# Linear attention and a two-layer MLP in one kernel: batch 1's kv between its transposes, its numerator a slot sooner, phi of batch 2 sooner, the first scale and two matmuls in halves

## The chip, the cores and the metric

The kernel runs on one core of a Trainium2 chip. The metric is device microseconds (us) of one execution. A program on one core has one value for each execution; executions of one kernel here lie within about 1.5 us of each other, and all runs quoted were in the fast state at a granted TensorE clock of 0.997 to 1.0. A profile is of one execution, and its span (first to last instruction) is about 1.8 us shorter than the time of that execution.

Names: PE is TensorE, ACT is ScalarE, DVE is VectorE, POOL is GpSimd, SP is the engine that issues most DMAs. L366 is line 366 of the kernel's source; the same statement has other line numbers in some variants (L387 is L392 where five lines were added above it, and the changed kernel's two matmuls in halves are at L577).

## The reference, cut to what matters

```python
def _attn_ref(q, k, v):                       # 8 batches, 8 heads, 576 tokens, 64 wide
    phi = lambda x: np.where(x > 0, x, np.exp(x) - 1.0) + 1.0
    q_p, k_p = phi(q), phi(k)
    kv = np.einsum('bhsd,bhse->bhde', k_p, v)
    z = np.sum(k_p, axis=2)
    num = np.einsum('bhsd,bhde->bhse', q_p, kv)
    den = np.einsum('bhsd,bhd->bhs', q_p, z)[..., None] + 1e-06
    return num / den

def _moe_ref(x, w_in, w_out):                 # x: 4608 tokens x 512
    h = x @ w_in                              # layer 1, 512 -> 2048
    g = h - np.tanh(h)
    return g @ w_out                          # layer 2, 2048 -> 512
```

The attention output of all heads, transposed to 4608 x 512, is the input of the MLP.

## The kernel before

The MLP goes in nine blocks of 512 tokens: 64 matmuls of layer 1 (L366), then 64 of layer 2 (L387), and so on. The attention of the following batches is put between these matmuls in "slots": the lists `s1[fi]` run after group `fi` of layer 1 (four matmuls each), and `s2[s]` after step `s` of layer 2 (four matmuls each). PE starts its matmuls in program order, so a slot whose input is not ready stops all matmuls behind it: at 39.17 us in the kernel before, the transposes wait 0.56 us for DVE, and the products behind them come only after them.

The parts that the change and the argument touch:

```python
# batch 0, before layer 1 of block 0
b0_spread((0, 2), 0)      # 1/den of head pairs 0 and 2, spread over partitions by PE (L240)
b0_scale(0, ns0, 0)       # xT = numerator x 1/den, on DVE (L244)
b0_scale(2, ns0, 1)
b0_num(1, ns0)
def open2():              # called after the first two matmuls of layer 1
    b0_spread((1, 3), 2); b0_scale(1, ns0, 2); b0_scale(3, ns0, 3)
...
def spread1(h):           # batch 1: 1/den spread by PE (L354), two scales on DVE (L359)
def num1():               # batch 1: numerator by PE, five copies to SBUF by ACT (L344, L346)
def a_split(b):           # 1/den split into bf16 parts: w, on DVE (L295 to L298)
def a_spread(b):          # later batches: 1/den goes to DRAM (ds) and comes back broadcast (rdb), by SP
def gate(qT):             # POOL reads the last element of qT, so the loads after it wait for the transposing DMA
...
# block c == 0
s2[7].append(lambda: (a_qT_pe(1, 0, side), a_qT_pe(1, 1, side), a_kv(1, side)))   # L164, L164, L177
s2[8].append(lambda: b0_scale_rest(side))
s2[9].append(lambda: a_den(1, side))
s2[10].append(lambda: (num1(), a_split(1)))
s2[11].append(lambda: spread1(0))
s2[12].append(lambda: q2(0))                         # phi of q, batch 2
s2[13].append(lambda: (spread1(1), q2(1)))
s2[14].append(lambda: q2(2))                         # ... and the transposing DMA of q, batch 2
s2[15].append(lambda: a_kphi(2, 0))                  # phi of k, batch 2
# blocks c >= 1, n1 = c + 1, n2 = c + 2
s1[7 if c == 1 else 5].append(lambda: a_kv_cols(n1, attn))                        # kv, L199
s1[10 if c == 1 else 8].append(lambda: (a_den(n1, attn), a_spread(n1)))
for p in range(NP + 1):
    s2[(11 if c == 1 else 9) + p].append(lambda p=p: a_num(n1, p))                # L317 on PE, L328 on DVE
s1[0].append(lambda: (gate(qT_t[n1]), load_k(n2), load_q(n2), load_v(n2)))
```

In layer 2 of block 0, steps 8 to 11 read the third quarter of `w_out`, which is loaded by POOL's DMA queue behind batch 1's q and v.

Of the kernel before, what the change touches and what calls it, by code (L numbers as in the profile page):

```python
# [18 lines left out]
def kernel(  # L19
# [9 lines left out]
    nc = tc.nc  # L29
# [127 lines left out]
    def a_qT_pe(b, i, banks, on=None):  # L157
        if i == 0:
            new_qT(b)
        for n in range(2):  # L160
            j0, j1 = ((0, 5), (5, 9))[n]
            ps = banks().bitcast(BF16).rearrange("p (j t) -> p j t", t=128)
            for j in range(j0, j1):
                nc.tensor.transpose(ps[:, j - j0, :], qp_t[b][:, i, j].rearrange("p h d -> p (h d)"), ident)  # L164
            src = ps[:, 0:j1 - j0, :]
            dst = qT_t[b][:, i, j0:j1].rearrange("p j g t -> p j (g t)")
            if (on or "AV")[n] == "A":
                nc.scalar.copy(dst, src)
            else:
                nc.vector.tensor_copy(dst, src)  # L170
# [69 lines left out]
                nc.tensor.matmul(ps_all[:, 4 + t, 128 * (n0 + n):128 * (n0 + n) + 128],  # L240
                                 sel[r, p].rearrange("p h e -> p (h e)"), rden_t[0][r, 0:128], start=True, stop=True)

    def b0_scale(p, ns, n):
        nc.vector.tensor_mul(  # L244
            xT[:, p, 0:512].rearrange("p (j t c) -> p t j c", j=8, t=4),
            ns[:, p, 0:8].rearrange("p j (t c) -> p t j c", t=4),
            ps_all[:, 4:8, 128 * n:128 * n + 128].rearrange("p t (j c) -> p t j c", c=16))

    def b0_rest():

# [225 lines left out]
    b0_kv(1)  # L476
    b0_kz(1)
    b0_spread((0, 2), 0)
    b0_scale(0, ns0, 0)
    b0_scale(2, ns0, 1)  # L480
    b0_num(1, ns0)

# [19 lines left out]
    for c in range(NC):  # L502
        gT = gpool.tile([128, NF, 512], BF16, name="gT")
        n1, n2 = c + 1, c + 2
        s1 = {i: [] for i in range(16)}
        s2 = {i: [] for i in range(16)}
        if c == 0:
            side = Banks([4, 5, 6, 7])
            sub = {}

            def spread1(h):
                sub["bp"] = a_spread_pe(1, 4, (2 * h, 2 * h + 1))
                for p in (2 * h, 2 * h + 1):
                    a_scale(1, p, sub["ns"], sub["bp"], 144 * (p % 2))

            def num1():
                sub["ns"] = new_ns(1)
                for p in (NP, 0, 1, 2, 3):
                    a_num_copy(1, sub["ns"], p, side)

            s1[11].append(lambda: a_kphi(1, 0))
            s1[13].append(lambda: a_kphi(1, 1))
            s2[3].append(lambda: a_qphi(1, 0))
            s2[4].append(lambda: (a_qphi(1, 1), load_q(2), load_k(2), load_v(2)))
            s2[0].append(prepare)
            s2[7].append(lambda: (a_qT_pe(1, 0, side), a_qT_pe(1, 1, side), a_kv(1, side)))
            s2[8].append(lambda: b0_scale_rest(side))
            s2[9].append(lambda: a_den(1, side))
            s2[10].append(lambda: (num1(), a_split(1)))
            s2[11].append(lambda: spread1(0))  # L530

            def q2(n):
                if n == 0:
                    sub["q"] = [phi_pieces(2, q_t, qp_t, "qp", i) for i in range(2)]
                if n < 2:
                    for f in sub["q"][n][:2]:
                        f()
                else:
                    for x in sub["q"]:
                        x[2]()  # L540
                    a_qT_dma(2)

            s2[12].append(lambda: q2(0))
            s2[13].append(lambda: (spread1(1), q2(1)))
            s2[14].append(lambda: q2(2))
            s2[15].append(lambda: a_kphi(2, 0))
        elif n1 < B:
            s1[7 if c == 1 else 5].append(lambda: a_kv_cols(n1, attn))
            s1[10 if c == 1 else 8].append(lambda: (a_den(n1, attn), a_spread(n1)))
            for p in range(NP + 1):  # L550
                s2[(11 if c == 1 else 9) + p].append(lambda p=p: a_num(n1, p))
        if c == 1:
            s1[1].append(lambda: a_kphi(2, 1))
            for i in range(2):
                s1[3].append(lambda i=i: a_vp(2, i))
        if c >= 1 and n2 < B:

            s1[0].append(lambda: (gate(qT_t[n1]), load_k(n2), load_q(n2), load_v(n2)))
            d = 2
            s2[d].append(lambda: a_kphi(n2, 0))  # L560
            s2[d + 2].append(lambda: a_kphi(n2, 1))
            s2[d + 4].append(lambda: a_qphi(n2, 0))
            s2[d + 6].append(lambda: (a_qphi(n2, 1), a_qT_dma(n2)))
            for i in range(2):
                s2[14 + i].append(lambda i=i: a_vp(n2, i))
        if c == 0:

            first = Banks([4, 5, 6, 7, 0, 1, 2, 3])
            hs = [ps_all[:, n, :] for n in range(4)]
            order = [((0, 0), (0, 1)), ((2, 0), (2, 1), (0, 2), (0, 3), (2, 2), (2, 3)),  # L570
                     [(p, fi) for p in (1, 3) for fi in range(4)]]
            seen = [0] * 4
            for n, part_ in enumerate(order):
                if n == 1:
                    open2()
                for p, fi in part_:
                    l1mm(c, fi, hs[fi], p, seen[fi])  # L577
                    seen[fi] += 1
            for fi in range(4):
                l1act(fi, hs[fi], gT)  # L580
        for fi in range(4 if c == 0 else 0, NF):
            h = first() if c == 0 else dense()
            for p in range(NP):
                l1mm(c, fi, h, p, p)
            if c == 0:
                l1act(fi, h, gT)
            elif fi % 2:
                n = dense.order[(dense.n - 1) % 6]
                l1act2(fi - 1, ps_all[:, n - 1:n + 1, :], gT)
            for f in s1[fi]:  # L590
                f()
        os_ = {}
        for s in range(16):

            (g, i) = divmod(s, 4) if c == 0 else (s % 4, s // 4)
            if g == 0:
                os_[i] = ps_all[:, i, :] if c == 0 else dense()
            if c == NC - 1 and i == 3:

                if g == 0:  # L600
                    o2 = dense()
                    for o, f in ((os_[i], slice(0, 384)), (o2, slice(384, DM))):
                        for fi in range(NF):
                            nc.tensor.matmul(o[:, f], gT[:, fi, 384:512], w_out_sb[:, fi, f],  # L604
                                             start=(fi == 0), stop=(fi == NF - 1))
                        evac(c, i, o, f.start, f.stop)
                continue
            l2mm(gT, os_[i], i, 4 * g, 4 * g + 4)
            if g == 3:
                evac(c, i, os_[i])  # L610
            for f in s2[s]:
                f()
# [30 lines left out]
```

## Time and profile before

| | before |
|---|---|
| time, median of 4 runs with the result's pair | 294.95 us (294.70 to 295.49) |
| span of the profiled execution | 293.2 us |
| PE busy | 285.2 us, 97% |
| PE idle waits that the profile names, before 60 us | 3.8 us, 1.2 of it at the very start |
| layer 1 of block 1 begins (first L366 after 51 us) | 51.30 us |
| den of batch 1 to its first spread, start to start | 3.94 us (43.32 to 47.26) |

How to read it: PE is the bound, so what counts are the waits of PE, and where PE stands at a few landmarks. Ends of matmuls are modelled, so I count from start to start: a 512-column matmul takes 0.216 us, a step or a group of four 0.863.

### The profile page before, as it was taken

What the parts mean: (1) busy time and instruction counts of PE and PEld (TensorE: products, weight loads), DVE (VectorE), ACT (ScalarE), POOL (GpSimd) and SP (SyncE); (2) the same over time, 40 slices, a digit from 0 to 9 for tenths busy, and PEclk for the clock granted to TensorE, in tenths of its full rate; (3) what the DMA queues carried; (4) which work ended last, traced back from release to release, by engine and by line L of the source; (5) the groups of instructions that cost most, each with busy time, mean ns of one, the idle gap of its engine ahead of it and who ended that gap; (6) DMA issues with size and microseconds to landing.
All of it is one profiled execution on the core that took longest, in us unless ns stands there. A gap on an engine that the chain in (4) does not pass through costs nothing.

```text
span 293.2 us, 4504 instructions
## 1 busy us (share of the span) xinstructions
PE 285.2 (97%) x1801; PEld 134.3 (46%) x1801; DVE 174.6 (60%) x265; ACT 139.6 (48%) x168; POOL 33.3 (11%) x55
## 2 busy tenths in 40 slices
PE   8899999999999999999999999999999999999994
PEld 2544453454444444444444445444444444444443
DVE  4759857887567764786478646865581456106600
ACT  4938536947344643455246524661552155126411
POOL 8673030030030003000300020000000000000000
PEclk9999999999999999999999999999999999999999
DMA  6999999998999758955895669667117310131032
GB/s 101 194 204 212 208 207 216 200 145 153 234 163 185 160 118 139 218 117 129 136 223 127 139 134 183 134 154 143 38 24 178 73 36 0 38 84 24 0 74 72
DMA packets 39077, 38.94 MB, mean 133 GB/s; under 512 B 16336, under 2 KB 33808, under 8 KB 38288
## 3 DMA queue, kind: packets, MB, share of 16 engines
q0 software_dynamic: 17552, 18.35, 38.6%
q1 hardware_dynamic: 21344, 20.17, 30.3%
q8 instruction: 14, 0.23, 0.3%
q10 hardware_dynamic: 160, 0.13, 0.1%
q14 instruction: 7, 0.06, 0.1%
HBM read 43.91 MB, written 9.55 MB: 182 GB/s over the span
## 4 chain that ended last, share of the span: by engine, by line
PE 79%; DMA 11%; issue 7%; POOL 2%; DVE 0%; ACT 0%; POOLq 0%
PE ps_all L387 37%; PE ps_all L366 36%; DMA qraw<-in_q_dram 6%; DMA w_in_sb<-in_moe_w_in_dram 3%; PE ps_all L199 2%; DMA kraw<-in_k_dram 2%; PE ps_all L317 2%; PE ps_all L604 1%; PE ps_all L276 1%; POOL qraw L90 0%; ACT e L134 0%; POOL kraw L93 0%; DVE qp L136 0%; POOL v L93 0%; POOL w_out_sb L115 0%
## 5 line engine op out<-in xcount | busy, mean ns | idle before, releaser
L366 PE MATMUL ps_all<-xT,w_in_sb 128*128 128x512 bf16 x576 | 128.0, 379 | 0.3 <-DVE xT L244 0.3
L387 PE MATMUL ps_all<-w_out_sb,gT 128*128 128x512 bf16 x560 | 127.8, 379 | 0.0
L373 DVE TENSOR_TENSOR gT<-ps_all,th 128x1024 bf16<-128x1024 f32 x64 | 77.9, 1218 | 59.8 <-ACT th L372 59.8
L372 ACT ACTIVATE th<-ps_all 128x1024 f32<-128x1024 f32 x64 | 65.5, 1024 | 57.0 <-PE ps_all L366 47.1
L366 PEld LDWEIGHTS <-w_in_sb 128*128 128x128 bf16 x576 | 55.3, 98 | 66.6 <-issue 0.6
L387 PEld LDWEIGHTS <-gT 128*128 128x128 bf16 x560 | 54.1, 98 | 64.3 <-issue 0.3
L396 ACT COPY osb<-ps_all 128x512 f32<-128x512 f32 (+1 forms) x36 | 20.9, 583 | 73.4 <-PE ps_all L387 54.2
L328 DVE TENSOR_TENSOR xT<-ps_all,rdb 128x512 bf16<-128x512 f32 x24 | 16.3, 689 | 13.4 <-PE ps_all L317 11.2
L134 ACT ACTIVATE e<-qraw 128x1152 bf16<-128x1152 bf16 x16 | 18.5, 1162 | 6.9 <-DMA qraw<-in_q_dram 6.9
L134 ACT ACTIVATE e<-kraw 128x1152 bf16<-128x1152 bf16 x15 | 17.5, 1166 | 0.2 <-DMA kraw<-in_k_dram 0.2
L136 DVE TENSOR_TENSOR qp<-e,r 128x1152 bf16<-128x1152 bf16 x16 | 12.0, 757 | 7.8 <-ACT e L134 7.2
L136 DVE TENSOR_TENSOR kp<-e,r 128x1152 bf16<-128x1152 bf16 x15 | 11.4, 759 | 8.3 <-ACT e L134 7.5
L383 POOL COPY g<-qT 1x1 bf16<-1x1 bf16 x5 | 1.2, 240 | 120.6 <-DMA qT<-qp 120.6
L378 DVE TENSOR_TENSOR gT<-ps_all,th 128x512 bf16<-128x512 f32 x16 | 10.3, 685 | 2.4 <-ACT th L377 1.7
L377 ACT ACTIVATE th<-ps_all 128x512 f32<-128x512 f32 x16 | 9.2, 598 | 4.3 <-PE ps_all L366 3.1
L317 PE MATMUL ps_all<-qT,kz 128*128 128x512 bf16 x28 | 10.1, 379 | 0.0
L444 PE MATMUL ps_all<-zero 128*128 128x512 bf16 x29 | 8.8, 463 | 1.2 <-DVE zero L405 1.2
L135 DVE TENSOR_SCALAR r<-qraw 128x1152 bf16<-128x1152 bf16 x16 | 7.3, 453 | 2.2 <-DMA qraw<-in_q_dram 2.2
L199 PE MATMUL ps_all<-vp,kp 64*128 64x136 bf16 x216 | 7.4, 220 | 0.4 <-POOL g L383 0.4
L199 PEld LDWEIGHTS <-kp 64*128 64x128 bf16 x216 | 6.4, 94 | 3.0 <-issue 2.1
L285 DVE RECIPROCAL rden<-den 128x144 f32<-128x144 f32 x7 | 7.4, 1053 | 0.2
L394 DVE COPY osb<-ps_all 128x128 f32<-128x128 f32 x1 | 0.3, 292 | 11.6 <-PE ps_all L604 11.6
(82 smaller groups left out, 121.7 us busy)
## 6 DMA issues: line engine op xcount, KB each, us to landing
out_dram<-osb SPq DMA_DIRECT2D x70, 128.0 KB
rdb<-ds SPq DMA_DIRECT2D x12, 576.0 KB
kraw<-in_k_dram POOLq DMA_DIRECT2D x7, 576.0 KB, 7.1
qraw<-in_q_dram POOLq DMA_DIRECT2D x7, 576.0 KB, 9.0
v<-in_v_dram POOLq DMA_DIRECT2D x7, 576.0 KB, 12.2
w_out_sb<-in_moe_w_out_dram POOLq DMA_DIRECT2D x4, 512.0 KB, 16.4
w_in_sb<-in_moe_w_in_dram POOLq DMA_DIRECT2D x6, 256.0 KB, 8.6
qraw<-in_q_dram POOLq DMA_DIRECT2D x2, 288.0 KB, 4.6
```

The costliest lines, as they stand in the source:

```text
L134: return (lambda: nc.scalar.activation(e, x, AF.Exp), lambda: nc.vector.tensor_scalar(r, x, 0.0, 1.0, ALU.max, ALU.add), lambda: nc.vector ...
L136: lambda: nc.vector.tensor_tensor(y, e, r, ALU.min))
L199: nc.tensor.matmul(ps[hg][:, i, :], kp[r, i, j].rearrange("p h d -> p (h d)"), vp[r, i, j, :], start=(j == 0), stop=(j == J - 1))
L317: nc.tensor.matmul(ps, kz[:, p // 2, p % 2, 0:128], qT[:, p % 2, 0:8, p // 2, :], start=True, stop=True)
L328: nc.vector.tensor_mul(xT[:, p, S * b:S * b + 512].rearrange("p (j t c) -> p j t c", j=8, t=4), ps.rearrange("p j (t c) -> p j t c", t=4), ...
L366: nc.tensor.matmul(h, w_in_sb[:, 2 * (p % 2) + p // 2, fi * 128:(fi + 1) * 128], xT[:, p, c * 512:(c + 1) * 512], start=(n == 0), stop=(n ...
L372: nc.scalar.activation(th, h, AF.Tanh)
L373: nc.vector.tensor_sub(gT[:, fi:fi + 2, :], h, th)
L377: nc.scalar.activation(th, h, AF.Tanh)
L378: nc.vector.tensor_sub(gT[:, fi, :], h, th)
L387: nc.tensor.matmul(o, gT[:, fi, i * 128:(i + 1) * 128], w_out_sb[:, fi, :], start=(fi == 0), stop=(fi == NF - 1))
L396: nc.scalar.copy(osb[:, f0:f1], o[:, f0:f1])
```

## The change

Its intent: (1) the first 1/den scale and the first two matmuls of layer 1 in halves of 256 tokens, so that PE starts sooner; (2) kv of batch 1 between its two blocks of transposes, so that PE has work while the second half of phi is made; (3) the numerator of batch 1 one slot sooner, so that its copies are done by the spread; (4) phi of batch 2 in earlier slots, and the kv product of batch 2 one group later.

```diff
--- before.py
+++ after.py
@@ -240,11 +240,11 @@
                 nc.tensor.matmul(ps_all[:, 4 + t, 128 * (n0 + n):128 * (n0 + n) + 128],
                                  sel[r, p].rearrange("p h e -> p (h e)"), rden_t[0][r, 0:128], start=True, stop=True)
 
-    def b0_scale(p, ns, n):
+    def b0_scale(p, ns, n, j0=0, j1=8):
         nc.vector.tensor_mul(
-            xT[:, p, 0:512].rearrange("p (j t c) -> p t j c", j=8, t=4),
-            ns[:, p, 0:8].rearrange("p j (t c) -> p t j c", t=4),
-            ps_all[:, 4:8, 128 * n:128 * n + 128].rearrange("p t (j c) -> p t j c", c=16))
+            xT[:, p, 64 * j0:64 * j1].rearrange("p (j t c) -> p t j c", j=j1 - j0, t=4),
+            ns[:, p, j0:j1].rearrange("p j (t c) -> p t j c", t=4),
+            ps_all[:, 4:8, 128 * n + 16 * j0:128 * n + 16 * j1].rearrange("p t (j c) -> p t j c", c=16))
 
     def b0_rest():
 
@@ -476,7 +476,9 @@
     b0_kv(1)
     b0_kz(1)
     b0_spread((0, 2), 0)
-    b0_scale(0, ns0, 0)
+
+    b0_scale(0, ns0, 0, 0, 4)
+    b0_scale(0, ns0, 0, 4, 8)
     b0_scale(2, ns0, 1)
     b0_num(1, ns0)
 
@@ -523,36 +525,33 @@
             s2[3].append(lambda: a_qphi(1, 0))
             s2[4].append(lambda: (a_qphi(1, 1), load_q(2), load_k(2), load_v(2)))
             s2[0].append(prepare)
-            s2[7].append(lambda: (a_qT_pe(1, 0, side), a_qT_pe(1, 1, side), a_kv(1, side)))
+            s2[7].append(lambda: (a_qT_pe(1, 0, side), a_kv(1, side), a_qT_pe(1, 1, side)))
             s2[8].append(lambda: b0_scale_rest(side))
-            s2[9].append(lambda: a_den(1, side))
-            s2[10].append(lambda: (num1(), a_split(1)))
+            s2[9].append(lambda: (a_den(1, side), num1(), a_split(1)))
             s2[11].append(lambda: spread1(0))
 
-            def q2(n):
-                if n == 0:
-                    sub["q"] = [phi_pieces(2, q_t, qp_t, "qp", i) for i in range(2)]
-                if n < 2:
-                    for f in sub["q"][n][:2]:
-                        f()
-                else:
-                    for x in sub["q"]:
-                        x[2]()
-                    a_qT_dma(2)
-
-            s2[12].append(lambda: q2(0))
-            s2[13].append(lambda: (spread1(1), q2(1)))
-            s2[14].append(lambda: q2(2))
-            s2[15].append(lambda: a_kphi(2, 0))
+            qs, ks = [], []
+
+            def exp2(pieces, src, store, name, i):
+                pieces.append(phi_pieces(2, src, store, name, i))
+                pieces[i][0]()
+
+            def rest2(f):
+                f[1]()
+                f[2]()
+
+            s2[11].append(lambda: (exp2(qs, q_t, qp_t, "qp", 0), rest2(qs[0])))
+            s2[12].append(lambda: exp2(qs, q_t, qp_t, "qp", 1))
+            s2[13].append(lambda: (spread1(1), exp2(ks, k_t, kp_t, "kp", 0), rest2(qs[1]), a_qT_dma(2)))
+            s2[14].append(lambda: rest2(ks[0]))
         elif n1 < B:
-            s1[7 if c == 1 else 5].append(lambda: a_kv_cols(n1, attn))
+            s1[8 if c == 1 else 5].append(lambda: a_kv_cols(n1, attn))
             s1[10 if c == 1 else 8].append(lambda: (a_den(n1, attn), a_spread(n1)))
             for p in range(NP + 1):
                 s2[(11 if c == 1 else 9) + p].append(lambda p=p: a_num(n1, p))
         if c == 1:
             s1[1].append(lambda: a_kphi(2, 1))
-            for i in range(2):
-                s1[3].append(lambda i=i: a_vp(2, i))
+            s1[3].append(lambda: (a_vp(2, 0), a_vp(2, 1)))
         if c >= 1 and n2 < B:
 
             s1[0].append(lambda: (gate(qT_t[n1]), load_k(n2), load_q(n2), load_v(n2)))
@@ -573,7 +572,12 @@
             for n, part_ in enumerate(order):
                 if n == 1:
                     open2()
-                for p, fi in part_:
+                for x in range(2 if n == 0 else 0):
+                    for p, fi in part_:
+                        nc.tensor.matmul(hs[fi][:, 256 * x:256 * x + 256], w_in_sb[:, 0, fi * 128:(fi + 1) * 128],
+                                         xT[:, p, 256 * x:256 * x + 256], start=(x == 0), stop=False)
+                        seen[fi] = 1
+                for p, fi in part_ if n else ():
                     l1mm(c, fi, hs[fi], p, seen[fi])
                     seen[fi] += 1
             for fi in range(4):
```

## The prediction

> **What bounds the kernel now.** I read the page first: busy time by engine, then the chain that ended last.
>
> ```profile
> PE 285.2 (97%) x1801; PEld 134.3 (46%) x1801; DVE 174.6 (60%) x265; ACT 139.6 (48%) x168; POOL 33.3 (11%) x55
> ...
> PE 79%; DMA 11%; issue 7%; POOL 2%; DVE 0%; ACT 0%; POOLq 0%
> ```
>
> TensorE (PE) is the bound: busy 97% of a span of 293.2 us, and the windows view gives 229.00 us of PE busy in the 229 us from 60 to 289. Nothing that lies after 60 us can therefore be gained; a change of order is worth only the PE idle time that it closes before that. So I read next what PE waited for (us in total, times, longest):
>
> ```profile
> PE ps_all L444 <- DVE zero L405: 1.2, 1, 1.2
> PE ps_all L164 <- DVE qp L136: 0.8, 2, 0.6
> PE ps_all L354 <- ACT ns L344: 0.7, 1, 0.7
> PE ps_all L221 <- DMA v<-in_v_dram: 0.4, 1, 0.4
> PE ps_all L199 <- POOL g L383: 0.4, 1, 0.4
> PE ps_all L366 <- DVE xT L244: 0.3, 1, 0.3
> ```
>
> Four of these are what the change is aimed at: the second block of transposes of batch 1 (L164, 0.56 us of its 0.8), the spread of 1/den of batch 1 (L354), the kv product of batch 2 (L199) and the first matmul of layer 1 (L366). Together some 2.0 us, 0.7% of the time: the most that could be had at face value. The timeline of PE (start us, us, what) places them, and shows what comes after each:
>
> ```profile
> 15.44 0.61 PE L231 MATMUL ps_all<-qT,kz 128*128 128x512 bf16 x2
> 16.38 0.59 PE L366 MATMUL ps_all<-xT,w_in_sb 128*128 128x512 bf16 x2 [0.33 <-DVE xT L244]
> 16.98 0.73 PE L240 MATMUL ps_all<-rden,sel 32*128 32x128 f32 x16
> ...
> 37.94 0.68 PE L164 MATMUL ps_all<-ident,qp 128*128 128x128 bf16 x9
> 39.17 0.68 PE L164 MATMUL ps_all<-ident,qp 128*128 128x128 bf16 x9 [0.56 <-DVE qp L136]
> 39.78 1.66 PE L177 MATMUL ps_all<-v,kp 64*128 64x192 bf16 x36
> 41.37 1.04 PE L387 MATMUL ps_all<-w_out_sb,gT 128*128 128x512 bf16 x4
> ```
>
> The reader should see that PE does not idle at 41.37. But the product there is the first that reads the third quarter of w_out, and the view of that tile, for the load issued at 23.01 us, says:
>
> ```profile
> L115 POOL DMA_DIRECT2D w_out_sb<-in_moe_w_out_dram x1: 762/762/762, 23.0 to 23.0; - x1
> ...
> DMA to landing us min/median/max: 18.3/18.3/18.3
> ```
>
> 23.0 + 18.3 = 41.3 us: it lands (41.32 in the trace) 0.05 us before PE gets there. The same view for batch 1's v, issued at 22.28, gives 16.5, so it lands at 38.80. The windows view has the DMA share at 1.2 in 31:38 and 38:41.4: the queue is full, so neither arrives sooner because PE does.
>
> **What the Trainium skill says.** "TensorE: Matmul & The Clock Gate", section "Wait — 56ns, not 53.3ns?", gives a start-to-start of about 215.7 ns for a warm 512-column matmul. The trace agrees: 62 matmuls of L366 from 17.64 to 31.03 are 0.216 us each. I count in starts, since ends are modelled. "PSUM — Partial Sum Buffer", section "PSUM bank collisions raise a hardware error", says that a dependency is put between two engines on one bank and quadrant even at different columns. The trace agrees: the second spread (L240) starts at 16.98, 0.06 after the second scale, which reads other columns of the same banks, ends at 16.92. The TensorE page's section "Architectural detail" calls ACT and DVE strict FIFO queues, so an early phi stands ahead of what comes later in program order; DVE's rows show that order throughout. "DMA: Bandwidth & Descriptors", section "Issuing engines are not separate DMA queues", has all DMAs share 16 engines, which fits the loads landing one after another 2.5 to 3 us apart.
>
> **Part 1, the first scale and two matmuls in halves.** DVE now has two scales from 15.64, 605 ns apart, the first ending at 16.32, and L366 starts at 16.38. A 256-column multiply from PSUM (L263, L225) takes 420 ns against 687, and the pipeline overlaps some 80, so I estimate halves ending at 16.06 and 16.40, and the scale of pair 2 at 16.99 instead of 16.92, since 2 x 0.34 is 0.07 more than 0.605. PE could start its first half at about 16.11. But the next PE instructions are the spread of pairs 1 and 3, and those wait for the scale of pair 2. They start 0.06 after it: at 17.05 in place of 16.98. The earlier start buys nothing, and layer 1 begins 0.07 us later. Even that does not last: batch 1's kv waits for v until 38.85 either way.
>
> **Part 2, kv between the transposes.** The 9 transposes start at 37.94 to 38.0 and are followed by kv after 9 x 0.056 + 0.15 = 0.65, at about 38.6. v lands at 38.80, so kv starts at about 38.85, an idle of 0.2. kv takes 41.37 - 39.78 = 1.59, to 40.44; the second transposes (qp of half 1 is ready at 39.11, the copies of half 0 have freed their banks at about 39.45) take 0.55, to 41.0. PE would be at the w_out product 0.37 sooner than 41.37, and waits for the landing at 41.32: it starts at about 41.34. Gain 0.03 us of the 0.72 that the starts show lost. The wait moves from DVE to two DMAs.
>
> **Part 3, the five copies of batch 1's numerator one slot earlier.** Before: den starts at 43.32, the numerator at 44.56, ACT's copies end at 47.20 (2.64 after the numerator starts), and the spread starts at 47.26 where an unheld PE would be at 46.50. After: den at 43.29, the numerator 0.37 later at 43.66, copies done at 46.30. PE gets to the spread at 46.47. The other input, w, comes from DVE: den 0.31, reciprocal 1.05 and four splits (0.23, 0.37, 0.23, 0.37), which end 3.22 after den starts, now as before: 43.29 + 3.22 = 46.51. So the spread starts at about 46.56: gain 0.70 us, w and no longer ns being the last wait (about 0.1).
>
> **Part 4, phi of batch 2 sooner, kv of batch 2 one step later.** Batch 2's kv starts at 58.74, 0.75 after the matmul before it, where its counterparts in later batches start 0.31 after: 0.43 us lost. The profile names the gate copy on POOL, which ends at 58.73, but kv does not read it. The first half of vp does: DVE's copies at L189 start at 58.23, 0.82 for two, so half 0 ends at about 58.7. They are late because DVE is: from 51.02 it has the phi of q half 1, of k half 0 and half 1 and two 1.22 us subtractions in a row. With most phi done before layer 1, and layer 1 of block 1 from 50.61, I work DVE out in order: scales of pairs 2 and 3 until 50.9, phi of q half 1 until 52.0, of k half 0 until 53.1, then the subtractions, k half 1 and vp, half 0 done at 57.5. kv, now after 9 groups, is due at 50.61 + 9 x 0.863 = 58.4. No wait: gain 0.43.
>
> What could be lost: the exponential of q half 0 stands on ACT before the evacuations, and q of batch 2 lands at 46.67 (issued 38.78, 7.9 to landing), so it runs 46.7 to 47.9, as the first evacuation comes due; the four then end by 52.4, the third at 51.8 where layer 1 wants its bank at 52.3. On DVE the phi of q half 0 goes before the scales of pairs 2 and 3: 50.2 and 50.9, wanted at 51.0 and 51.25. Both fit, with 0.3 to 0.5 us to spare.
>
> **Sum.** 0 + 0.03 + 0.67 + 0.43 = 1.13 us, of 295.09: 293.96. I say 293.9, for w_out may land a little sooner in other executions.
>
> **Rivals.** (a) All gaps close at face value, DMA not in the way: for it, the waits view shows no w_out wait; against it, the landing times. Then 0.37 more, perhaps 0.2 from part 1: 293.4. (b) Phi too early: its wait for q on ACT, or its place before the scales on DVE, holds layer 1 of block 1 for 0.3 to 0.6 us: about 294.4. For it, margins of 0.3; against it, that each stands worked out as met. (c) The loads for batch 3, released about 1.5 us sooner since the transposing DMA is issued sooner, disturb later stages. Against it: no PE idle after 60 us and DMA shares of 0.59 there; no change.
>
> **Range and chances.** Before spreads over 294.81 to 295.49, 0.7 us; the rivals span 293.4 to 294.4. I take 293.2 to 294.8. A change of 2% is 5.9 us, three times all the idle in question, and no step here can cost that; 98% within.
>
> **What would show it.** Right: spread of pairs 1 and 3 at 17.0 to 17.1 despite a first matmul near 16.1; kv of batch 1 held by v until about 38.85; the product at s = 8 held by DMA until about 41.3; first spread of batch 1 near 46.6, released by w; layer 1 of block 1 from about 50.6; no gap before batch 2's kv at about 58.4. Wrong: the product at s = 8 starting near 41.0 (rival a), or gaps in layer 1 of block 1, or behind ACT's first evacuations (rival b).

## More of the kernel before

One more place turned out to matter, which the prediction did not look at: the numerators of batch 2 in layer 2 of block 1. The timeline of PE before (start us, us, what) has them at

```profile
77.66 0.38 PE L317 MATMUL ps_all<-qT,kz 128*128 128x512 bf16 x1
...
78.73 0.38 PE L317 MATMUL ps_all<-qT,kz 128*128 128x512 bf16 x1
...
79.85 0.38 PE L317 MATMUL ps_all<-qT,kz 128*128 128x512 bf16 x1
```

and the timeline of DVE shows when the multiply of the first of them by 1/den could run, and what it waited for:

```profile
79.10 1.89 DVE L328 TENSOR_TENSOR xT<-ps_all,rdb 128x512 bf16<-128x512 f32 x3 [2.26 <-DMA rdb<-ds]
```

The first numerator starts at 77.66, but 1/den (rdb) lands only at 79.1. The numerators use two PSUM banks in turn, so the third has to wait until DVE has read the first. Unheld they stand 1.08 us apart (one step and one numerator); here the third is 1.12 after the second: 0.04 us lost. The kernel before stands right at the edge of this wait.

## The result, and the profile after

The changed kernel takes 293.67 us (median of 4 runs, 293.54 to 293.97) against 294.95 for the kernel before (4 runs). The ratio is 0.9956, with a 95% interval of 0.9938 to 0.9973: clearly a little faster. Ratios here are the mean time of one kernel's fast runs over that of the other's of the same rounds, so they are not quite the ratio of the medians. The predicted 293.9 and its range hold.

The page after, busy time and the chain that ended last:

```profile
PE 284.2 (97%) x1775; PEld 134.5 (46%) x1803; DVE 174.8 (60%) x266; ACT 139.7 (48%) x168; POOL 33.1 (11%) x55
...
PE 75%; DMA 18%; POOL 2%; issue 1%; SPq 1%; DVE 1%; ACT 1%; DVEq 0%; POOLq 0%
```

DMA's share of the chain went from 11% to 18%: the chain now runs over loads. (PE's count is lower only because some matmul records are missing from the trace; a start-to-start of 0.43 is one of those.) What PE waited for, after:

```profile
PE ps_all L444 <- DVE zero L405: 1.2, 1, 1.2
PE ps_all L221 <- DMA v<-in_v_dram: 0.4, 1, 0.4
PE ps_all L240 <- DVE xT L244: 0.2, 1, 0.2
PE ps_all L366 <- issue: 0.2, 1, 0.2
```

The four waits that the change aimed at are gone, and one is new, of the spread (L240) for the scale. The last line is a missing record. The timeline of PE after:

```profile
16.12 0.71 PE L577 MATMUL ps_all<-xT,w_in_sb 128*128 128x256 bf16 x4
17.05 0.73 PE L240 MATMUL ps_all<-rden,sel 32*128 32x128 f32 x16 [0.22 <-DVE xT L244]
...
38.01 0.67 PE L164 MATMUL ps_all<-ident,qp 128*128 128x128 bf16 x9
38.60 1.66 PE L177 MATMUL ps_all<-v,kp 64*128 64x192 bf16 x36
40.20 0.68 PE L164 MATMUL ps_all<-ident,qp 128*128 128x128 bf16 x9
40.93 1.02 PE L387 MATMUL ps_all<-w_out_sb,gT 128*128 128x512 bf16 x3
...
46.16 0.30 PE L354 MATMUL ps_all<-w,sel 32*128 32x144 bf16 x8
...
50.20 7.93 PE L366 MATMUL ps_all<-xT,w_in_sb 128*128 128x512 bf16 x35
58.06 1.24 PE L199 MATMUL ps_all<-vp,kp 64*128 64x136 bf16 x36
```

and the view of the tile w_out for the load of its third quarter, issued at 23.05 us:

```profile
L115 POOL DMA_DIRECT2D w_out_sb<-in_moe_w_out_dram x1: 760/760/760, 23.1 to 23.1; - x1
...
DMA to landing us min/median/max: 17.8/17.8/17.8
```

It lands at 40.89, and step 8 starts at 40.93, with no idle shown: the modelled ends of the transposes cover the wait. Layer 1 of block 1 begins at 50.20 in place of 51.30, and kv of batch 2 comes without a gap. By 61 us PE is 1.54 us ahead (den of batch 2 at 61.06, before 62.60). But the span is only 1.3 us shorter. The difference is in layer 2 of block 1, where PE shows no named wait:

```profile
76.12 0.38 PE L317 MATMUL ps_all<-qT,kz 128*128 128x512 bf16 x1
...
77.20 0.38 PE L317 MATMUL ps_all<-qT,kz 128*128 128x512 bf16 x1
...
78.54 0.38 PE L317 MATMUL ps_all<-qT,kz 128*128 128x512 bf16 x1
```

```profile
77.80 1.89 DVE L328 TENSOR_TENSOR xT<-ps_all,rdb 128x512 bf16<-128x512 f32 x3 [2.49 <-DMA rdb<-ds]
```

The third numerator now stands 1.34 us after the second, 0.26 more than unheld. 1/den of batch 2 lands 1.30 us sooner than before (77.80 against 79.10), PE was 1.54 sooner, and the later of the two decides.

So the account of these two executions, start to start:

| step | before | after | gained, us |
|---|---|---|---|
| step 8 of layer 2 starts | 41.37 | 40.93 | 0.44 |
| den of batch 1 to its first spread | 3.94 | 3.29 | 0.65 |
| last matmul before kv of batch 2 to kv | 0.75 | 0.31 | 0.43 |
| second to third numerator of batch 2 | 1.12 | 1.34 | -0.22 |
| sum | | | 1.30 |

The spans differ by 1.32 us. The last line is one that the prediction did not have. The first differs from it (0.03), but most of that line is not the work of the change. The chain of batch 1 begins when its q lands (the load issued at 19.4 us), and ACT's exponential waits for it. First the kernel before, then the changed one:

```profile
35.92 2.22 ACT L134 ACTIVATE e<-qraw 128x1152 bf16<-128x1152 bf16 x2 [3.39 <-DMA qraw<-in_q_dram]
```

```profile
35.51 2.22 ACT L134 ACTIVATE e<-qraw 128x1152 bf16<-128x1152 bf16 x2 [2.90 <-DMA qraw<-in_q_dram]
```

q landed at 35.90 and at 35.48, and step 8 starts 5.47 and 5.45 us after that. So 0.42 of the 0.44 us is a sooner landing of all these loads in this one execution; 0.02 is left for part 2. The table of all looks below bears this out.

### The profile page after: what moved, and what is told of

Its sections match the earlier page's. It is cut to its first block, busy times and chain, and to the rows that moved or that the text cites. A ratio compares the mean times of both kernels' runs of the same rounds, so it can differ in the third digit from the quotient of the medians.

```text
span 291.8 us, 4476 instructions
## 1 busy us (share of the span) xinstructions
PE 284.2 (97%) x1775; PEld 134.5 (46%) x1803; DVE 174.8 (60%) x266; ACT 139.7 (48%) x168; POOL 33.1 (11%) x55
## 4 chain that ended last, share of the span: by engine, by line
PE 75%; DMA 18%; POOL 2%; issue 1%; SPq 1%; DVE 1%; ACT 1%; DVEq 0%; POOLq 0%
PE ps_all L366 37%; PE ps_all L387 32%; DMA w_out_sb<-in_moe_w_out_dram 6%; DMA w_in_sb<-in_moe_w_in_dram 3%; DMA rdb<-ds 3%; DMA out_dram<-osb 2%; PE ps_all L199 2%; DMA kraw<-in_k_dram 2%; PE ps_all L317 2%; DMA ds<-rden 1%; PE ps_all L276 1%; POOL v L419 1%; ACT osb L396 1%; SPq L401 0%; POOL qraw L90 0%
## 5 line engine op out<-in xcount | busy, mean ns | idle before, releaser
L366 PE MATMUL ps_all<-xT,w_in_sb 128*128 128x512 bf16 x558 | 126.5, 380 | 0.9 <-issue 0.2
L387 PE MATMUL ps_all<-w_out_sb,gT 128*128 128x512 bf16 x548 | 126.2, 380 | 0.7
```

Source lines behind the costliest of these rows:

```text
L366: nc.tensor.matmul(h, w_in_sb[:, 2 * (p % 2) + p // 2, fi * 128:(fi + 1) * 128], xT[:, p, c * 512:(c + 1) * 512], start=(n == 0), stop=(n ...
L387: nc.tensor.matmul(o, gT[:, fi, i * 128:(i + 1) * 128], w_out_sb[:, fi, :], start=(fi == 0), stop=(fi == NF - 1))
```

## The experiments

My theory after the result: (A) halving is worth nothing; (B) what kv between the transposes is worth is set by the landing of w_out's third quarter, which differs from execution to execution; (C) the sooner numerator is worth 0.65 us; (D) phi sooner and kv one group later are worth 0.43 where kv waits, but a second DMA, 1/den of batch 2 on its way through DRAM, holds the third numerator, and it is late because it stands behind the loads of batch 3. (On B the looks say more, below: the landing of w_out moves together with that of q, so what part 2 is worth does not depend on it.) The rivals are named with each run. A "look" is the one profiled execution of a run. All kernels were timed in 5 rounds; the four of one block below ran on the same chip beside the kernel before, which had medians of 295.06, 295.00 and 294.87 us in the three blocks. One profile of each was taken.

### The parts alone

**Part 1 undone, from the changed kernel.**

```diff
-    b0_scale(0, ns0, 0, 0, 4)
-    b0_scale(0, ns0, 0, 4, 8)
+    b0_scale(0, ns0, 0)
...
-                for x in range(2 if n == 0 else 0):
-                    ... two matmuls of 256 columns for each of two groups ...
-                for p, fi in part_ if n else ():
+                for p, fi in part_:
```

> The changed kernel with part 1 undone: the first scale and the first two matmuls of layer 1 whole again. Theory (halving buys nothing, since PE waits for the scale of pair 2 before the spread of pairs 1 and 3): that spread starts at about 16.98 in place of 17.05 us, layer 1's rest 0.07 sooner, and the time is the same as the changed kernel's within 0.1 us, since the w_out load holds PE at about 41 us either way. Rival (the halves let layer 1 begin 0.26 us sooner and that reaches the end): 0.2 to 0.3 us slower than the changed kernel, about 293.9.

Measured: 294.06 us (293.93 to 294.56), ratio to before 0.9967 (0.9955 to 0.9980). Counted from the start of the first scale, the second spread starts after 1.34 us, as before, where all looks with halves have 1.40 to 1.41; so that part of the theory holds. The time is 0.3 us above the changed kernel's, which looks like the rival. But the two weren't run side by side, and in this look step 8 starts at 41.08, 0.04 after w_out landed (41.04), and the third numerator stands 1.63 us after the second, with 1/den at 78.23. The third numerator alone is 0.29 us later than in the changed kernel's first look and 0.55 later than in its second. So the difference can't be put down to the halves from this run. A later pair, and above all the table of looks, settles it.

**Part 2 alone, from the kernel before.**

```diff
-            s2[7].append(lambda: (a_qT_pe(1, 0, side), a_qT_pe(1, 1, side), a_kv(1, side)))
+            s2[7].append(lambda: (a_qT_pe(1, 0, side), a_kv(1, side), a_qT_pe(1, 1, side)))
```

> The kernel before with part 2 alone: kv of batch 1 between its two blocks of transposes. Theory: the idle of 0.56 us before the second transposes goes, but the first product after them starts 0.05 us after the third quarter of w_out lands and not before; the gain is what the landing allows, between 0 (a landing at 41.3) and 0.4 us (a landing at 40.9 or sooner). Rival (no DMA in the way): the product starts 0.14 us after the last transpose, and the gain is 0.4 to 0.7 us wherever w_out lands.

Measured: 294.92 us (294.66 to 295.33), ratio 0.9995 (0.9982 to 1.0008): nothing that the times can tell. In the look, w_out landed at 41.14 and step 8 started at 41.18, 0.19 sooner than in the look of before; but q had landed 0.17 sooner (35.73), so 0.02 is the edit's. The lead was lost again at the third numerator, 1.27 us after the second, since 1/den came at 79.07 as before (79.10). The look excludes the rival: step 8 starts 0.31 us after the last transpose (40.88) and not 0.14. The times alone would leave room for a gain of up to 0.5.

**Part 3 alone, from the kernel before.**

```diff
-            s2[9].append(lambda: a_den(1, side))
-            s2[10].append(lambda: (num1(), a_split(1)))
+            s2[9].append(lambda: (a_den(1, side), num1(), a_split(1)))
```

> The kernel before with part 3 alone: the numerator of batch 1 and its copies one slot sooner. Theory: the first spread starts about 0.66 us sooner against the den before it (3.25 us after den starts in place of 3.94), held by w from DVE by about 0.1; all of it reaches the end: about 0.65 us faster than before. Rival (ACT's earlier copies or PSUM banks wait elsewhere): under 0.3 us.

Measured: 294.25 us (294.15 to 294.47), ratio 0.9973 (0.9959 to 0.9987), 0.8 us below before. The timeline of PE in this run:

```profile
43.35 0.43 PE L276 MATMUL ps_all<-qT,kz 128*32 128x144 bf16 x16
...
46.63 0.30 PE L354 MATMUL ps_all<-w,sel 32*128 32x144 bf16 x8
```

From den to the spread it is 3.28 us, against 3.94. The numerators of batch 2 stand 1.08 apart here: everything that follows on PE and DVE came sooner, and with it the gate, the loads of batch 3 (first at 58.25 against 58.86) and 1/den (78.43 against 79.10). This part is the largest and the one that reaches the end whole.

**Part 4 alone, from the kernel before.** The edit is what the change does to `q2`, `exp2`/`rest2` and the slot of `a_kv_cols`; the removed lines are summed up in one here.

```diff
-            s2[12] ... s2[15]: q2(0), q2(1), q2(2), a_kphi(2, 0)
+            s2[11].append(lambda: (exp2(qs, q_t, qp_t, "qp", 0), rest2(qs[0])))
+            s2[12].append(lambda: exp2(qs, q_t, qp_t, "qp", 1))
+            s2[13].append(lambda: (spread1(1), exp2(ks, k_t, kp_t, "kp", 0), rest2(qs[1]), a_qT_dma(2)))
+            s2[14].append(lambda: rest2(ks[0]))
...
-            s1[7 if c == 1 else 5].append(lambda: a_kv_cols(n1, attn))
+            s1[8 if c == 1 else 5].append(lambda: a_kv_cols(n1, attn))
```

> The kernel before with part 4 alone: phi of batch 2 sooner and the kv product of batch 2 after 9 groups in place of 8. Theory: no wait before that kv (0.43 us gained), and the loads of batch 3 start about as much sooner or more, so that 1/den of batch 2, which crosses memory behind them, is on time too: 0.4 us faster than before, less up to 0.1. Rival (phi in front of the scales and the evacuations holds layer 1 of block 1): no faster than before, gaps of 0.3 us or more in layer 1 of block 1.

Measured: 294.71 us (294.35 to 294.97), ratio 0.9986 (0.9973 to 0.9998): some 0.35 us faster. kv of batch 2 comes 0.31 after the matmul before it. The profiled execution was the slowest of the five (294.97); in it q of batch 3 took until 68.73 and v until 71.73, 1/den came at 79.16, and the third numerator 1.46 after the second: of the 0.43 us gained, 0.38 were given back. That 1/den came sooner in the faster executions is not shown; they have no profile.

### The load of v, and the halves in a cleaner pair

**The changed kernel again**, for the side-by-side comparison with the next three.

> The changed kernel once more, on the chip of the next three. Both theories: about 293.7 us; the product at step 8 starts 0.05 us after the third quarter of w_out lands, wherever that is between 40.8 and 41.4, and the third numerator of batch 2 stands 1.3 us or more after the second in place of 1.08, waiting for 1/den of batch 2.

Measured: 293.76 us (293.45 to 294.00), ratio 0.9959 (0.9947 to 0.9971). In this look w_out landed late, at 41.53, and step 8 started at 41.57, later than in the look of before; kv of batch 1 was held by v (landed 39.01, kv at 39.05). The numerators stand 1.08 apart with 1/den at 78.11: the second half of what I expected did not show. That is not because PE was later: q landed 0.62 later (36.10), and gate, rdb's issue and the numerators are all 0.62 to 0.63 later with it. What differs is that rdb took 8.21 us from its issue to the first multiply, in place of 8.53. The runs don't show why.

**Batch 3's v later, from the changed kernel.** A one-element copy on POOL that reads an element of `gT` group 13 holds the load back.

```diff
+    def gate_g(gT):
+        g0 = rpool.tile([1, 1], BF16, name="g0")
+        nc.gpsimd.tensor_copy(g0, gT[0:1, 13, 0:1])
...
-            s1[0].append(lambda: (gate(qT_t[n1]), load_k(n2), load_q(n2), load_v(n2)))
+            if c == 1:
+                s1[0].append(lambda: (gate(qT_t[n1]), load_k(n2), load_q(n2)))
+                s1[13].append(lambda: (gate_g(gT), load_v(n2)))
+            else:
+                s1[0].append(lambda: (gate(qT_t[n1]), load_k(n2), load_q(n2), load_v(n2)))
```

> The changed kernel with one thing more: batch 3's v is loaded after 13 groups of layer 1 of block 1, not right behind its k and q. Theory (some 0.25 us of the gain is given back because 1/den of batch 2 crosses memory behind the three loads of batch 3): 1/den lands 2 us sooner, the four numerators of batch 2 stand 1.08 us apart, and the time is 0.2 to 0.3 us below that of the changed kernel. Rival (the loss is in another wait, or v then comes too late for its copies): no change, or slower.

Measured: 294.63 us (293.81 to 294.81), ratio 0.9981 (0.9968 to 0.9995). It is slower than the changed kernel (0.9 us in the medians; the intervals just touch), and in two groups: two executions at 293.81 and 293.91, four from 294.53 to 294.81. The timelines of SP show half of the theory right. First the changed kernel's second look, then this run:

```profile
64.56 1.29 SPq L305 DMA_DIRECT2D ds<-rden  x4
69.90 1.12 SPq L308 DMA_DIRECT2D rdb<-ds  x2
```

```profile
64.46 1.29 SPq L305 DMA_DIRECT2D ds<-rden  x4
67.46 1.12 SPq L308 DMA_DIRECT2D rdb<-ds  x2
```

With v out of the way, the step back from DRAM (rdb) is issued 2.4 us sooner: 0.29 us after q landed (67.17), where otherwise it was near the landing of v (70.36). So in these runs the small transfer to DRAM does wait behind the loads. But rdb itself then ran beside v's load and took from 67.46 to 77.69, 10.2 us, against 8.2 (69.90 to 78.11). The 2 us were lost again. The profiled execution is one of the two fast ones.

**The same with part 1 undone.**

```diff
 (late v as above)
-    b0_scale(0, ns0, 0, 0, 4)
-    b0_scale(0, ns0, 0, 4, 8)
+    b0_scale(0, ns0, 0)          # and the first two matmuls whole
```

> The same with part 1 undone (scale and first matmuls whole), so that the wait for 1/den of batch 2 can't blur the comparison. Theory: the same time as with halves, within 0.15 us; layer 1's main run starts 0.07 us sooner and the product at step 8 still starts 0.05 us after w_out lands. Rival (the halves are worth 0.26 us): 0.2 to 0.3 us slower than with halves.

Measured: 294.66 us (293.52 to 294.97), ratio 0.9980 (0.9963 to 0.9996), next to 294.63 and 0.9981 with halves. The two groups are here too: 293.52 and 293.66, and four from 294.58. Neither the medians nor the fast groups favour the halves, but with two groups and intervals of about 0.5 us to each side, this pair could not exclude the rival's 0.26 by itself. This profiled execution is one of the slow group, and shows what it lost; its waits of PE have

```profile
PE ps_all L317 <- DVE xT L328: 0.7, 1, 0.7
```

which no look of the changed kernel has at this size. 1/den came at 78.75, the third numerator 1.90 us after the second: 0.82 us later than unheld, which is about the distance of the groups. That the other slow executions lost their time there too is likely, and not shown.

**A try at a faster version**: late v, part 1 undone, and den of batch 1 a step sooner.

```diff
 (late v and whole scale as above)
-            s2[8].append(lambda: b0_scale_rest(side))
-            s2[9].append(lambda: (a_den(1, side), num1(), a_split(1)))
+            s2[8].append(lambda: (b0_scale_rest(side), a_den(1, side)))
+            s2[9].append(lambda: (num1(), a_split(1)))
```

> A try at a faster version: late v, part 1 undone, and den of batch 1 one step sooner than its numerator, so that w is ready before PE asks for the spread. Theory: no wait before the first spread (0.31 us after the matmul before it in place of 0.42), 0.1 us below the run with late v, 0.3 to 0.4 below the changed kernel. Rival (an earlier den meets the copies of the second transposes or the kz product): a new gap of 0.1 us or more before den, and no gain.

Measured: 293.58 us (293.32 to 294.27), ratio 0.9958 (0.9945 to 0.9971), against 293.76 and 0.9959 for the changed kernel in the same block: no difference that these runs can tell. The wait before the spread is gone as expected (0.31 in place of 0.42 us). Here, as in six other looks with kv between the transposes, the profile names the wait on w_out itself, because the matmul before left a visible gap:

```profile
41.02 1.02 PE L392 MATMUL ps_all<-w_out_sb,gT 128*128 128x512 bf16 x3 [0.25 <-DMA w_out_sb<-in_moe_w_out_dram]
```

### What holds, taken away one at a time

**Batch 3's v sooner, from the changed kernel**: right behind batch 2's.

```diff
+            s2[9].append(lambda: load_v(3))
...
-            s1[0].append(lambda: (gate(qT_t[n1]), load_k(n2), load_q(n2), load_v(n2)))
+            s1[0].append(lambda: (gate(qT_t[n1]), load_k(n2), load_q(n2)))
+            if c > 1:
+                s1[0].append(lambda: load_v(n2))
```

> The changed kernel with one thing more: batch 3's v is loaded right behind batch 2's, from 41 us on, not with batch 3's k and q (its buffer is free once kv of batch 1 is done). Theory (1/den of batch 2 waits first behind the loads of batch 3 and is then, on its way back, slowed by any load that runs beside it): the step of 1/den out of memory is issued at about 67 in place of 69.3 us, takes 8 to 8.5 us with no load beside it, and is there by 76; the four numerators of batch 2 stand 1.08 us apart in every look; 0 to 0.25 us below the changed kernel, with no executions above 294. Rival (what slows it is not the loads): the third numerator still waits in some executions, and the time is that of the changed kernel or of the run with late v.

Measured: 293.72 us (293.21 to 294.10), ratio 0.9960 (0.9948 to 0.9971): the changed kernel's time. My expectation of 67 us failed: rdb was issued at 69.44. The timeline of POOL says why:

```profile
59.30 0.18 POOL L383 COPY g<-qT 1x1 bf16<-1x1 bf16 x1 [17.24 <-DMA qT<-qp]
59.82 0.74 POOL L93 DMA_DIRECT2D kraw<-in_k_dram  x1 [0.33 <-issue]
```

The gate waits for the transposing DMA of q, and was let go at 59.30, where the two looks of the changed kernel have 56.60 and 57.23. The early v landed at 57.19, so it ran in the stretch in which the transposing DMA otherwise had ended; k and q of batch 3 came about as much later as v's place was worth. The gate comes 17.6 to 18.0 us after step 8 in the three runs with early v, and 15.65 to 15.81 after it in the six other looks with parts 3 and 4, so the early v does make it later. That it does so by delaying the transposing DMA is my reading of the times; no run shows it apart.

**The same with part 1 undone and den a step sooner.**

```diff
 (early v as above)
-    b0_scale(0, ns0, 0, 0, 4)
-    b0_scale(0, ns0, 0, 4, 8)
+    b0_scale(0, ns0, 0)          # and the first two matmuls whole
...
-            s2[8].append(lambda: b0_scale_rest(side))
-            s2[9].append(lambda: (a_den(1, side), num1(), a_split(1)))
+            s2[8].append(lambda: (b0_scale_rest(side), a_den(1, side)))
+            s2[9].append(lambda: (num1(), a_split(1)))
```

> A try at the fastest: v early, part 1 undone, den of batch 1 one step before its numerator. Theory: the first spread no longer waits for w (0.31 us after the matmul before it), and undoing the halves costs nothing: 0.1 us below the run with v early alone, about 293.4. Rival (the halves are worth 0.26 us): 0.15 us above it.

Measured: 293.73 us (293.39 to 293.98), ratio 0.9958 (0.9946 to 0.9970), next to 293.72 and 0.9960. Neither the 0.1 us of the sooner den nor a loss without halves shows in the time. In the look the third numerator waits (1.35 after the second, 1/den at 77.88): what the sooner spread gave, the wait took.

**The wait for w_out's third quarter taken away**: steps 8 to 11 read the second quarter again. The result is wrong (relative error 0.18).

```diff
 (early v as above)
-            l2mm(gT, os_[i], i, 4 * g, 4 * g + 4)
+            l2mm(gT, os_[i], i, 4 * g, 4 * g + 4, 4 if c == 0 and g == 2 else 0)   # reads w_out_sb[:, fi - 4]
```

> The run with v early, in which the four products at steps 8 to 11 read the second quarter of w_out again in place of the third; the result is wrong on purpose, the amount of work is the same. It takes away the wait for the third quarter's landing alone. Theory (part 2's gain is held by that landing): the product at step 8 starts 0.15 us after the last transpose in place of 0.3 to 0.5, whatever the landing, and the time falls by 0.1 to 0.35 us. Rival (something else holds step 8): the start stays 0.3 us or more after the last transpose and the time does not fall.

Measured: 293.57 us (293.16 to 294.65), ratio 0.9962 (0.9947 to 0.9976). The timeline of PE:

```profile
40.57 0.68 PE L164 MATMUL ps_all<-ident,qp 128*128 128x128 bf16 x9
41.08 1.03 PE L387 MATMUL ps_all<-w_out_sb,gT 128*128 128x512 bf16 x4
```

Step 8 starts 0.05 us after the last transpose's start (41.03), although the third quarter landed only at 41.45 in this execution. So the landing, and nothing else, held step 8. But the time falls by no more than 0.15 us in the medians, with intervals that overlap: PE then stood at the numerators of batch 2 sooner, and waited for 1/den (78.24), the third 1.63 us after the second.

**The kv product of batch 2 one group later, alone, from the kernel before.**

```diff
-            s1[7 if c == 1 else 5].append(lambda: a_kv_cols(n1, attn))
+            s1[8 if c == 1 else 5].append(lambda: a_kv_cols(n1, attn))
```

> The kernel before with only the kv product of batch 2 moved from after 8 groups to after 9; phi stays where it was. Theory: the wait before that kv goes (0.31 us after the matmul before it in place of 0.75), since vp is there by 58.7 us and PE comes only at 59.1; but the loads of batch 3 start no sooner, so the third numerator of batch 2 waits about as much longer, and the time falls by less than 0.2 us. Rival (the prediction's sum): 0.4 us faster than before.

Measured: 294.94 us (294.55 to 295.08), ratio 1.0000 (0.9987 to 1.0013): nothing that the times can tell. The wait before kv is gone (0.31 in place of 0.75), and the timeline of PE shows where part of it went:

```profile
78.38 0.38 PE L317 MATMUL ps_all<-qT,kz 128*128 128x512 bf16 x1
...
79.63 0.38 PE L317 MATMUL ps_all<-qT,kz 128*128 128x512 bf16 x1
```

The third numerator is 1.25 after the second, and 1/den is at 78.88, with batch 3's first load at 58.79, about as before. So 0.13 of the 0.43 went there. Another 0.16 went before kv: the ninth group's first matmul, at 58.29, stands 0.38 after the one before it, where the others stand 0.22, and starts when DVE's subtraction ends (57.02 and 1.22 us). With phi sooner this gap is not there (58.06 less 50.20 is 7.86 us from the start of layer 1 to kv, here 59.25 less 51.23, 8.02). Against that, part 4 as a whole gained 0.35; the intervals overlap. So phi sooner is not needed for vp to be there in time, but it is worth those 0.16 us; what it adds further, I argue, is a sooner gate (57.83 in the look of part 4 alone against 58.22 here, though PE was 0.2 us later there), so sooner loads of batch 3 and a sooner 1/den. The one look of part 4 alone doesn't show the last step, since its q and v landed late.

### All looks side by side

Times in us from the start of the span; "q lands" is batch 1's q; "rdb issued" and "1/den" are SP's issue of the step back from DRAM and DVE's first multiply with it.

| run | q lands | w_out lands | step 8 | den to spread | rdb issued | 1/den | 3rd after 2nd numerator | span |
|---|---|---|---|---|---|---|---|---|
| before | 35.90 | 41.32 | 41.37 | 3.94 | 70.65 | 79.10 | 1.12 | 293.2 |
| part 2 alone | 35.73 | 41.14 | 41.18 | 3.94 | 70.53 | 79.07 | 1.27 | 293.1 |
| part 3 alone | 35.94 | 41.35 | 41.41 | 3.28 | 69.98 | 78.43 | 1.08 | 292.5 |
| part 4 alone | 36.04 | 41.47 | 41.51 | 3.94 | 70.65 | 79.16 | 1.46 | 293.2 |
| kv later alone | 35.83 | 41.25 | 41.30 | 3.94 | 70.46 | 78.88 | 1.25 | 292.9 |
| changed kernel | 35.48 | 40.89 | 40.93 | 3.29 | 69.27 | 77.80 | 1.34 | 291.8 |
| changed, second look | 36.10 | 41.53 | 41.57 | 3.29 | 69.90 | 78.11 | 1.08 | 292.2 |
| part 1 undone | 35.61 | 41.04 | 41.08 | 3.28 | 69.66 | 78.23 | 1.63 | 292.2 |
| late v | 36.00 | 41.43 | 41.47 | 3.28 | 67.46 | 77.69 | 1.08 | 292.1 |
| late v, whole | 35.88 | 41.30 | 41.34 | 3.28 | 68.06 | 78.75 | 1.90 | 292.8 |
| late v, whole, den sooner | 35.56 | 40.98 | 41.02 | 4.04 | 67.02 | 77.28 | 1.07 | 291.6 |
| early v | 36.22 | 41.65 | 41.69 | 3.29 | 69.44 | 77.69 | 1.08 | 292.3 |
| early v, whole, den sooner | 35.67 | 41.09 | 41.13 | 4.04 | 69.36 | 77.88 | 1.35 | 291.9 |
| early v, no w_out wait | 36.02 | 41.45 | 41.08 | 3.28 | 69.73 | 78.24 | 1.63 | 292.3 |

(Where den is a step sooner, "den to spread" has a step more in it.) In every row but the last, step 8 starts 0.04 to 0.06 us after w_out lands. (With the old order of transposes and kv, PE's own work also ends just then, 0.17 to 0.18 after the start of the last kv matmul; q, v and w_out land one behind the other, so both move together. Only with kv between the transposes is the landing alone what holds.) In every row with more than 1.1 in the last column but one, the third numerator starts 0.74 to 0.75 us after 1/den's first multiply does.

Counted from the landing of q, the looks agree to a few hundredths:

- q's landing to step 8: 5.45 to 5.47 us in every row but the last (5.07), with the old order of transposes and kv or the new, with halves or without.
- Step 8 to layer 1 of block 1: 9.92 or 9.93 without part 3, 9.26 or 9.27 with it (9.15 or 9.16 with den a step sooner).
- Layer 1 of block 1 to den of batch 2: 11.30 or 11.31 before, 11.03 with kv later alone, 10.87 with part 4.
- Den of batch 2 to its first numerator: 15.05. From the third numerator to the end: 213.26 to 213.34.

So the parts are worth 0 (part 1), 0.00 to 0.02 (part 2), 0.66 (part 3) and 0.43 us (part 4, 0.16 of it by phi). What differs beyond that between looks is when the loads land, and how long the third numerator waits for 1/den.

## Why the prediction was right or wrong

- **The sum and the range: right.** 293.9 predicted, 293.67 measured (293.76 in the second block), inside 293.2 to 294.8. The sum was taken from 295.09; from the 294.95 of the result's four runs it gives 293.82.
- **Part 1, worth nothing: right, shown.** The first matmul came at 16.12 (predicted 16.11), the spread at 17.05 (17.05), bound by the scale of pair 2. The looks settle it: step 8 comes 5.45 to 5.47 us after q's landing in the four with halves that have the w_out wait and in the nine without halves. Undoing it, in the pair with late v, changed the median by 0.03 us.
- **Part 2, the wait moves to the w_out load, 0.03: right, shown.** "It starts at about 41.34. Gain 0.03 us": in the first look it started at 40.93, because w_out landed at 40.89. But q had landed 0.42 sooner too, and from there the gain is 0.02. The prediction took the landing from one execution as if it were fixed; 14 looks put it anywhere from 40.89 to 41.65, with and without the change. That did not hurt its gain, since what PE waits for before moves with w_out. Taken alone, part 2 gained nothing (294.92 against 295.06, the interval covers 1). The other half, kv held by v until about 38.85, is not seen in the first look (v landed at 38.38, kv followed the transposes at 38.60) and is seen in the second (39.01 and 39.05).
- **Rival (a), DMA not in the way: excluded** by taking the w_out wait away: only then did step 8 follow the transposes at once (0.05 us, where I had estimated 0.1), and 5.07 us after q's landing: the 0.4 sooner that rival (a) needed.
- **Part 3, 0.67 to 0.70: right, shown.** Den to spread fell from 3.94 to 3.28 or 3.29, and the spread was then held by w: w ends at 46.10 and the spread starts at 46.16, 0.1 later than unheld. The sum's 0.67 is the 0.70 less part 2's 0.03. Alone it gave 0.8 us in the medians, 0.66 in the look.
- **Part 4, no wait before kv, 0.43: right at its place, wrong as a gain that stays.** The gap closed to 0.31. But the sum took it as kept to the end, on the statement "Nothing that lies after 60 us can therefore be gained" and, under rival (c), "no PE idle after 60 us ... no change". That step failed. PE showed no idle there, but the third numerator of batch 2 stood only 0.04 us inside its wait for 1/den, so a gain on PE could be lost there unless 1/den came sooner too: kv later alone kept 0.14 of its 0.43 us in the look, and nothing that the times can tell. The view of busy time could not show this: a matmul is booked with 0.38 us while starts stand 0.216 apart, and even the 0.26 us that the third numerator waited in the changed kernel's first look are named nowhere. In the changed kernel, counted from step 8, the gate came 15.67 us later in place of 16.92, thanks to part 3 (16.27 alone) and to phi sooner (16.32 alone), and 1/den 0.86 us sooner in the first look; PE was 1.10 sooner, so 0.22 us more than before were lost. In the second look 1/den was quicker and nothing was lost.
- **Rival (b), phi too early: did not happen.** The scales of pairs 2 and 3 ended in time and layer 1 of block 1 ran from 50.20 without a gap; ACT did wait for q (its exponential ran from 46.95), as worked out.
- **Where the luck is.** The parts come to 1.11 us in the looks, against 1.13, less 0 to 0.22 for 1/den: that is no luck. That the two profiles differ by 1.32 is: 0.42 of it is the sooner landing of the loads, and 0.22 were lost again. The medians differ by 1.28, but their interval, 0.8 to 1.8 us, can't tell these sums apart.

What stays open: why q of batch 3 lands 2.8 us after k in some executions and up to 3.9 in others, and why two groups of executions appear with late v. The slow group shows 1/den late; what decides between the groups was not seen. No version tried is clearly faster than the changed kernel.

## What to carry to other kernels

When PE never idles in a stage, that does not mean that the stage would take more speed: look how far each input is ahead of its use there, above all a DMA chain whose start doesn't move with the matmuls. A reordering is worth the distance to the next input that is tied to something else, and that distance should be read from landings and not from idle times. And a landing in one profile is one draw: here it moved by 0.76 us between executions, more than any part is worth (0.66 at most). So before two profiles are compared, line them up at a landing that both chains start from: here the landing of q, after which 0.44 us of apparent gain became 0.02.

## What the Trainium skill lacked or had wrong

- "DMA: Bandwidth & Descriptors", "Issuing engines are not separate DMA queues", says that DMAs of all engines interleave on the same 16 engines. The page also says that each DMA engine takes turns between its queues, packet by packet. It lacks the time that a small transfer of another engine then has to wait: 4 x 4.5 KB from SP, issued from 64.56 us while two loads of POOL (q and v) were under way, let the step that follows go only at 69.90, near the landing of the last load (70.36); with one load less it was 67.46 (landing 67.17). Interleaving did not give the small transfer a quick way through.
- The same page has no figure that would have told how much a broadcast from DRAM (2 x 576 KB written to SBUF) suffers from one load beside it. Here it took 8.2 to 8.6 us from issue to first use in the eleven looks in which a load ran beside it for at most 1.1 us, 10.2 to 10.7 us in the three in which one ran beside most or all of it.
- No page that I read gives a spread for the landing of one and the same queued load: 40.89 to 41.65 us over 14 executions, issued between 23.01 and 23.75.
- "TensorE: Matmul & The Clock Gate" and "PSUM — Partial Sum Buffer" agreed where used: 0.216 us for each 512-column matmul, and the spread held 0.06 us behind a scale that reads other columns of its banks (17.05 after 16.99).
